# A six-layer cross network on one core: biases transposed by VectorE, remainder loads on two queues, first layer by column groups

## The chip, the core and the metric

The kernel runs on one core of one Trainium2 chip. TensorE (PE) multiplies into eight banks of PSUM (128 partitions x 512 fp32 each); ScalarE (ACT), VectorE (DVE) and GpSimd (POOL) work element by element; transfers are issued from SyncE's queue (SP) or ACT's. Each engine takes its instructions in the order in which the program gives them. The metric is the time of the launch on the device in microseconds (us), the median of several runs; all times below are us.

## What is computed

```python
B, F, D, L = 4096, 26, 16, 6
Din = min(F * D, 1024)          # 416
x0: (B, Din)   ws: (L, Din, Din)   bs: (L, Din)      # all bf16

def reference(x0, ws, bs):
    x = x0
    for l in range(ws.shape[0]):
        x = x0 * (x @ ws[l] + bs[l]) + x
    return x
```

In layer 0, x is x0, so x0 * (x0 @ w + b) + x0 is x0 * (x0 @ w + (b + 1)): the kernel adds 1 to the first layer's bias and leaves the addition out.

## The kernel before, in words

**Layout.** The 416 columns are three blocks of 128 (`NK`, index m for outputs and k for inputs) and a remainder of 32. x is held transposed: `XM[i][:, k, batch]` for the blocks, and `XR[i]` for the remainder, where the 32 columns of four groups of 512 rows lie on the four quarters of the partitions. The 4096 rows are two halves s of 2048, each of four groups of `CW` = 512 (index g). A unit of PE work in the first layer is three matmuls (k) of 128x128 by 128x512 for one output block m and one group: `full` (L222, the matmul on L225). The remainder's part is added by `row` (L228, L232), which multiplies 32 partitions of `XR[0]`, or of `XRx`, a copy with the two 64-partition halves swapped, so that four such matmuls use the four quarters of the array beside each other.

**Loads.** `load_x0t` (L78) fetches 512 rows transposed by DMA, eight times, on SP. `load_xrem` (L83) fetches the 32 remainder columns, 64 bytes a row; those of s = 0 in two pieces of 64 partitions, the first from ACT's queue behind the weights of layer 0 (L99), the second from SP behind the fourth transposed load (L106); those of s = 1 whole (L109). `x0_rem` (L157) makes `XR[0]` and `XRx` of them on DVE: a transpose in 32x32 squares, a copy that reorders, one copy per 64 partitions for `XRx`. All later weights, the rows of x0 for the last layer (`X0rows`, four issues) and the last bias (`bLr`, four issues) follow on SP.

**Biases.** `bias_setup` (L143) transposes the 6x416 biases on PE with an identity matrix that POOL makes (L91): three matmuls and four more for the remainder, into bank 7. DVE adds 1 to the first layer's and copies them to `bM` and `bR` (L151 to L154). ACT reads them per partition.

**Order on PE.** `pe_filler` (L136) runs matmuls on a constant tile from the start: two of 256 columns, nine of 512, then the bias matmuls, and one more of 512. The first layer (`first_layer`, L219) follows for s = 0 and s = 1. A block's result of two groups (one half h of the four) takes a pair of banks, which `two_banks` (L131) hands out in turn, 0, 1, 2, 3. In s = 0, h = 0 goes by groups: (m, group) = (0,0), (1,0), (2,0), (0,1), (1,1), (2,1); h = 1 goes block by block. Six row matmuls close a half. The results of h = 0 are called `pa[m]`, those of h = 1 `pb[m]`.

**Eviction.** `ew_main` (L165) is called for a block and half: ACT reads both banks at once (128x1024), adds the bias and writes bf16 (L168); DVE multiplies by x0 (L171 in layer 0; L173 and L174, with the addition, later). PE may use the pair again when ACT has read it. The remainder's own output is `mm_rem` (L200) and `ew_rem` (L176).

**Later.** Layers 1 to 4 (L300) take six tiles (s, m) of two bank pairs each in the same manner; layer 5 (L385) multiplies with x as the stationary side, so that results come out by rows, and stores them.

Of the kernel before, what the change touches and what calls it, by code (L numbers as in the profile page):

```python
# [16 lines left out]
def kernel(  # L17
# [7 lines left out]
    nc = tc.nc  # L25
# [24 lines left out]
    ident = const.tile([P, P], BF16)  # L50
# [6 lines left out]
    bsb = const.tile([L, D], BF16)  # L57
# [82 lines left out]
    pe_filler(2, 2 * P)  # L140
    pe_filler(9, CW)

    def bias_setup():  # L143
        pb = PS[:, 7, 0:32].rearrange("p (a b) -> p a b", a=4)
        for m in range(NK):
            nc.tensor.matmul(pb[:, m, 0:L], lhsT=bsb[0:L, 128 * m:128 * m + 128], rhs=ident[0:L, 0:L], start=True, stop=True,
                             skip_group_check=True)
        for g in range(NG):
            nc.tensor.matmul(pb[32 * g:32 * g + 32, 3, 0:L], lhsT=bsb[0:L, NK * P:D], rhs=ident[0:L, 0:L], start=True, stop=True,
                             tile_position=(0, 32 * g), skip_group_check=True)  # L150
        nc.vector.tensor_scalar(out=bM[:, :, 0:1], in0=pb[:, 0:NK, 0:1], scalar1=1.0, scalar2=None, op0=ALU.add)  # L151
        nc.vector.tensor_scalar(out=bR[:, 0:1], in0=pb[:, 3, 0:1], scalar1=1.0, scalar2=None, op0=ALU.add)
        nc.vector.tensor_copy(bM[:, :, 1:L], pb[:, 0:NK, 1:L])
        nc.vector.tensor_copy(bR[:, 1:L], pb[:, 3, 1:L])  # L154


    def x0_rem(s, p0, p1):  # L157
        nc.vector.transpose(out=xrt[s][p0:p1], in_=xrem[s][p0:p1])  # L158
        nc.vector.tensor_copy(XR[0][p0:p1, CW * s:CW * s + CW].rearrange("p (j t) -> p j t", t=16),
                              xrt[s][p0:p1].rearrange("p t j -> p j t"))  # L160
        for a in range(p0, p1, 64):
            nc.vector.tensor_copy(XRx[s][64 - a:128 - a, :], XR[0][a:a + 64, CW * s:CW * s + CW])


    def ew_main(l, s, m, h, pt, cur, nxt):  # L165
        c0 = col0(s, 2 * h)
        t = tpool.tile([P, 2 * CW], BF16, name="t")
        nc.scalar.activation(t[:], pt.rearrange("p a b -> p (a b)"), ACT.Identity, bias=bM[:, m, l:l + 1], scale=1.0)  # L168
        x0c = XM[0][:, m, c0:c0 + 2 * CW]
        if l == 0:  # L170
            nc.vector.tensor_tensor(out=nxt[:, m, c0:c0 + 2 * CW], in0=t[:], in1=x0c, op=ALU.mult)  # L171
# [47 lines left out]
    def first_layer(s):  # L219
# [31 lines left out]
        for m in range(NK):  # L251
            ew_main(0, s, m, 0, pa[m], cur, nxt)
        for gl in range(2):
            full(pb[0], 0, 1, gl, s == 0, s == 1)
        if s == 1:
            ew_main(0, s, 0, 1, pb[0], cur, nxt)
        for m in range(1, NK):
            pb.append(two_banks())
            for gl in range(2):
                full(pb[m], m, 1, gl, True, False)  # L260
        if s == 0:
# [3 lines left out]
            x0_rem(1, 0, 128)  # L265
            for m in range(NK):
# [170 lines left out]
```

## Time and profile before

| | us |
|---|---|
| median of three runs (131.67 to 131.97) | 131.84 |
| the profiled execution | 131.1 |
| its span, first to last instruction | 129.3 |
| PE busy | 122.5 |
| DVE busy | 103.1 |
| ACT busy | 83.9 |
| first matmul of the first layer starts | 5.64 |
| first matmul of layer 1 starts | 26.36 |
| last matmul of layer 5 is issued in the piece that ends at | 122.83 |

Times in the rows count from the start of the span. A row of the timeline has start, length, engine, line, operation, output and inputs, and in brackets the idle time of the engine before it and what released it. PEld is the loading of weights into PE; SPq and ACTq are issues of transfers. A row of the groups has the count, the busy time, the mean length in ns, and the idle time before with its releaser.

### The profile page before, as it was taken

To read this page: it belongs to the slowest core of one execution; us is meant where nothing else is said; L and a number is where in the kernel's file an instruction comes from. 1 tells how busy PE (TensorE), PEld (TensorE's weight loads), DVE (VectorE), ACT (ScalarE), POOL (GpSimd) and SP (SyncE) were. 2 spreads that over 40 slices of the span, in tenths; PEclk is the share of its full clock that TensorE was granted. 3 is DMA by queue.
4 is the path that set the end of the run, shared out by engine and by line. 5 is a ranking of instruction groups with operands and counts; after the bars stand their busy time and mean duration, and the time that the engine had idled before them with its cause. 6 is when DMAs were issued, how large, how long until landed. Compare 5 with 4: busy or idle time off the path is not lost.

```text
span 129.3 us, 3927 instructions
## 1 busy us (share of the span) xinstructions
PE 122.5 (95%) x1681; PEld 54.4 (42%) x1683; DVE 103.1 (80%) x186; ACT 83.9 (65%) x92; POOL 5.4 (4%) x18
## 2 busy tenths in 40 slices
PE   6989999999999999999999999999999999999940
PEld 2433343444544444434444544444444345544420
DVE  1163768547989898989898989898989999999990
ACT  0307567598757759756759666849665867567760
POOL 4110000300000000000000000000001200000000
PEclk9999999999999999999999999999999999999997
DMA  3999999999990000000000000000499899996553
GB/s 93 254 213 200 159 182 261 232 329 333 334 298 8 5 0 8 0 0 5 0 5 0 5 0 5 0 5 0 82 126 193 162 138 231 225 312 198 191 172 101
DMA packets 42021, 16.37 MB, mean 127 GB/s; under 512 B 30826, under 2 KB 42004, under 8 KB 42004
## 3 DMA queue, kind: packets, MB, share of 16 engines
q1 hardware_dynamic: 40504, 15.70, 54.5%
q10 hardware_dynamic: 1500, 0.42, 1.7%
q8 instruction: 13, 0.21, 0.7%
q14 instruction: 4, 0.03, 0.1%
HBM read 6.15 MB, written 3.41 MB: 74 GB/s over the span
## 4 chain that ended last, share of the span: by engine, by line
PE 88%; DMA 5%; DVE 1%; ACT 1%; SPq 1%; issue 1%; DVEq 0%
PE PS L190 49%; PE PS L342 12%; PE PS L225 10%; PE PS L196 5%; PE PS L207 5%; DMA XM<-in_x_dram 5%; PE PS L202 2%; PE PS L351 2%; PE PS L232 1%; PE PS L356 1%; SPq L78 1%; DVE t L377 1%; ACT t L168 1%; DVE o L380 1%; ACT t L376 0%
## 5 line engine op out<-in xcount | busy, mean ns | idle before, releaser
L168 ACT ACTIVATE t<-PS,bM 128x1024 bf16<-128x1024 f32 x60 | 62.1, 1114 | 30.8 <-PE PS L196 21.3
L190 PE MATMUL PS<-XM,WM 128*32 128x512 bf16 x1152 | 65.2, 379 | 0.0
L190 PEld LDWEIGHTS <-WM 128*32 128x32 bf16 x1152 | 29.7, 97 | 33.8 <-issue 5.1
L173 DVE TENSOR_TENSOR t<-t,XM 128x1024 bf16<-128x1024 bf16 x48 | 33.3, 694 | 4.2 <-ACT t L168 4.2
L174 DVE TENSOR_TENSOR XM<-t,XM 128x1024 bf16<-128x1024 bf16 x48 | 33.5, 699 | 3.1
L342 PE MATMUL PS<-WM,XM 128*128 128x416 bf16 x96 | 17.9, 340 | 0.0
L225 PE MATMUL PS<-XM,WM 128*128 128x512 bf16 x70 | 16.6, 379 | 0.7 <-DMA XM<-in_x_dram 0.4
L366 ACT CAST t<-PS 128x832 bf16<-128x832 f32 x12 | 10.2, 852 | 5.0 <-PE PS L342 2.5
L342 PEld LDWEIGHTS <-XM 128*128 128x128 bf16 x96 | 8.9, 98 | 8.7 <-issue 2.2
L225 PEld LDWEIGHTS <-WM 128*128 128x128 bf16 x72 | 6.8, 98 | 10.1 <-issue 2.7
L171 DVE TENSOR_TENSOR XM<-t,XM 128x1024 bf16<-128x1024 bf16 x12 | 7.9, 689 | 2.3 <-ACT t L168 2.1
L207 PE MATMUL PS<-XM,WM 128*32 128x512 bf16 x120 | 8.2, 379 | 0.0
L178 ACT ACTIVATE t<-PS,bR 128x512 bf16<-128x512 f32 x10 | 6.8, 694 | 1.4 <-PE PS L207 1.4
L368 DVE TENSOR_TENSOR o<-t,XLrows 128x832 bf16<-128x832 bf16 x12 | 7.1, 592 | 0.5
L196 PE MATMUL PS<-XR,WR 32*128 32x512 bf16 x96 | 7.3, 379 | 0.0
L367 DVE TENSOR_TENSOR t<-t,X0rows 128x832 bf16<-128x832 bf16 x12 | 7.0, 584 | 0.0
L158 DVE STREAM_TRANSPOSE xrt<-xrem 64x512 bf16<-64x512 bf16 (+1 forms) x3 | 2.1, 708 | 5.0 <-DMA xrem<-in_x_dram 5.0
L138 PE MATMUL PS<-warm 128*128 128x512 bf16 (+1 forms) x12 | 4.4, 536 | 1.2 <-DVE warm L89 1.2
L376 ACT CAST t<-PS 128x416 bf16<-128x416 f32 x8 | 4.0, 505 | 1.0 <-PE PS L342 0.8
L207 PEld LDWEIGHTS <-WM 128*32 128x32 bf16 x120 | 3.2, 97 | 3.2
L285 POOL COPY XLrows<-scrR 128x512 bf16<-128x512 bf16 x2 | 1.4, 704 | 74.1 <-DMA scrR<-XR 74.1
L102 DVE COPY WR<-WR 32x416 bf16<-32x416 bf16 x3 | 0.8, 259 | 4.5 <-DMA WR<-in_ws_dram 4.4
(39 smaller groups left out, 42.2 us busy)
## 6 DMA issues: line engine op xcount, KB each, us to landing
X0rows<-in_x_dram SPq DMA_DIRECT2D x4, 832.0 KB, 10.6
out_dram<-o SPq DMA_DIRECT2D x12, 208.0 KB, 2.5
WM<-in_ws_dram SPq DMA_DIRECT2D x5, 312.0 KB
out_dram<-o SPq DMA_DIRECT2D x8, 104.0 KB, 1.8
WR<-in_ws_dram SPq DMA_DIRECT2D x4, 130.0 KB, 5.3
WM<-in_ws_dram ACTq DMA_DIRECT2D x1, 312.0 KB, 3.3
XM<-in_x_dram SPq DMA_TRANSPOSE x8, 4.8
xrem<-in_x_dram SPq DMA_DIRECT2D x1, 128.0 KB
```

The source lines that it names most:

```text
L168: nc.scalar.activation(t[:], pt.rearrange("p a b -> p (a b)"), ACT.Identity, bias=bM[:, m, l:l + 1], scale=1.0)
L171: nc.vector.tensor_tensor(out=nxt[:, m, c0:c0 + 2 * CW], in0=t[:], in1=x0c, op=ALU.mult)
L173: nc.vector.tensor_tensor(out=t[:], in0=t[:], in1=x0c, op=ALU.mult)
L174: nc.vector.tensor_tensor(out=nxt[:, m, c0:c0 + 2 * CW], in0=t[:], in1=cur[:, m, c0:c0 + 2 * CW], op=ALU.add)
L190: nc.tensor.matmul(pts[g // 2][32 * q:32 * q + 32, g % 2, :], lhsT=WM[:, l, k, 128 * m + 32 * q:128 * m + 32 * q + 32], rhs=cur[:, k, c0:c ...
L196: nc.tensor.matmul(pts[g // 2][:, g % 2, :], lhsT=WR[32 * g:32 * g + 32, l, 128 * m:128 * m + 128], rhs=curR[32 * g:32 * g + 32, CW * s:CW ...
L207: nc.tensor.matmul(pr[32 * g:32 * g + 32, :], lhsT=WM[:, l, k, NK * P:D], rhs=cur[:, k, c0:c0 + CW], start=False, stop=(k == NK - 1), tile ...
L225: nc.tensor.matmul(pt[:, gl, :], lhsT=WM[:, 0, k, 128 * m:128 * m + 128], rhs=cur[:, k, c0:c0 + CW], start=(first and k == 0), stop=(last ...
L342: nc.tensor.matmul(py[g // 2][:, g % 2, 0:D], lhsT=cur[:, k, q_cols(q, g)], rhs=WM[:, l, k, :], start=(first and k == 0), stop=((not first ...
L366: nc.scalar.copy(tv, py[h][:, :, 0:D])
L367: nc.vector.tensor_tensor(out=tv, in0=tv, in1=X0rows[:, b0:b0 + 5:4, :], op=ALU.mult)
L368: nc.vector.tensor_tensor(out=o[:], in0=tv, in1=XLrows[:, b0:b0 + 5:4, :], op=ALU.add)
```

## The change

- **Biases.** `bsb` grows to 32 partitions, POOL zeroes it, the biases are loaded into its first six. DVE transposes it in 32x32 squares into `bT`; POOL copies from there to `bM` (four copies) and `bR` (four) and adds 1 to the first layer's. The identity, `bias_setup` and the filler behind it go.
- **Loads.** The first half of the remainder rows of s = 0 is issued by SP as third transfer, behind two transposed loads. The second half is issued by ACT behind its part of the first `x0_rem`. `X0rows` and `bLr` are one issue each.
- **`x0_rem`** takes a list of engines: the first half of s = 0 is transposed and reordered in two pieces, one copy on ACT and one on DVE.
- **First layer.** h = 1 of s = 0 goes by groups as h = 0 does. The rows are closed in the order 0, 2, 1 and the blocks evicted in that order. In s = 1, h = 1 takes (0,0), (1,0), (0,1), (1,1), (2,0), (2,1) and evicts block 0 in between. The bank pairs follow a list, `first_order`, and then the turn 2, 1, 3, 0.
- **`split_first`** evicts block 0 of a half by two engines: ACT the first bank as before, DVE the second bank directly, (PSUM + bias) * x0 in one operation; DVE's multiply for ACT's half is 512 columns. It is used for h = 0 of both s, and for h = 1 of s = 0.
- **Fillers.** Three of 128 columns, nine of 512, one of 256; the constant tile is filled in pieces of 128 and 384 columns.

```diff
-    bsb = const.tile([L, D], BF16)
+    bsb = const.tile([R, D], BF16)
+    bT = const.tile([R, D // R, R], BF16)
...
-    make_identity(nc, ident[:])
+    nc.gpsimd.memset(bsb[:], 0.0)
...
-    nc.scalar.dma_start(bsb[:], bs[:, :])
+    nc.scalar.dma_start(bsb[0:L, :], bs[:, :])
     load_wr(nc.scalar, 0, 0, 1)
-    load_xrem(nc.scalar, 0, 0, 64)
     nc.scalar.activation(dz[:, 1:2], dz[:, 0:1], ACT.Identity, bias=dz[:, 0:1], scale=1.0)
+    nc.vector.transpose(out=bT[:], in_=bsb.rearrange("p (c r) -> p c r", r=R))
+    for q in range(4):
+        nc.gpsimd.tensor_copy(bM[32 * q:32 * q + 32, :, :], bT[:, q:4 * NK:4, 0:L])
+    nc.gpsimd.tensor_scalar(out=bM[:, :, 0:1], in0=bM[:, :, 0:1], scalar1=1.0, scalar2=None, op0=ALU.add)
+    for g in range(NG):
+        nc.gpsimd.tensor_copy(bR[32 * g:32 * g + 32, :], bT[:, 4 * NK, 0:L])
+    nc.gpsimd.tensor_scalar(out=bR[:, 0:1], in0=bR[:, 0:1], scalar1=1.0, scalar2=None, op0=ALU.add)
     for g in range(1, NG):
         nc.vector.tensor_copy(WR[32 * g:32 * g + 32, 0, :], WR[0:32, 0, :])
     load_x0t(0, 1)
+    load_xrem(nc.sync, 0, 0, 64)
     load_x0t(0, 2)
     load_x0t(0, 3)
-    load_xrem(nc.sync, 0, 64, 128)
     load_x0t(1, 0)
     load_x0t(1, 1)
     load_xrem(nc.sync, 1, 0, 128)
...
-    for q in range(4):
-        nc.sync.dma_start(X0rows[:, 8 * q:8 * q + 8, :], x0_v[:, 8 * q:8 * q + 8, :])
-    for g in range(NG):
-        nc.sync.dma_start(bLr[32 * g:32 * g + 1, :], bs[LL:LL + 1, :])
+    nc.sync.dma_start(X0rows[:], x0_v)
+    nc.sync.dma_start(bLr[0:P:32, :], bs[LL:LL + 1, :].broadcast_to([NG, D]))
...
+    first_order = [0, 1, 2, 3, 0, 2, 1, 3, 0, 2, 1, 0, 3]
     def two_banks():
-        i = 2 * (turn[0] % 4)
+        n = turn[0]
+        i = first_order[n] if n < len(first_order) else (2, 1, 3, 0)[(n - len(first_order)) % 4]
         turn[0] += 1
-        return PS[:, i:i + 2, :]
+        return PS[:, 2 * i:2 * i + 2, :]
...
-    pe_filler(2, 2 * P)
+    pe_filler(3, P)
     pe_filler(9, CW)
-    def bias_setup():
...
+    pe_filler(1, 2 * P)
-    def x0_rem(s, p0, p1):
-        nc.vector.transpose(out=xrt[s][p0:p1], in_=xrem[s][p0:p1])
-        nc.vector.tensor_copy(XR[0][p0:p1, CW * s:CW * s + CW].rearrange("p (j t) -> p j t", t=16),
-                              xrt[s][p0:p1].rearrange("p t j -> p j t"))
+    def x0_rem(s, p0, p1, parts):
+        XRv = XR[0][p0:p1, CW * s:CW * s + CW].rearrange("p (j t) -> p j t", t=16)
+        n = 16 // len(parts)
+        for a, copy in enumerate(parts):
+            nc.vector.transpose(out=xrt[s][p0:p1, n * a:n * a + n, :], in_=xrem[s][p0:p1, n * a:n * a + n, :])
+            copy(XRv[:, :, n * a:n * a + n], xrt[s][p0:p1, n * a:n * a + n, :].rearrange("p t j -> p j t"))
         for a in range(p0, p1, 64):
             nc.vector.tensor_copy(XRx[s][64 - a:128 - a, :], XR[0][a:a + 64, CW * s:CW * s + CW])
...
+    def split_first(s, m, h, pt, nxt):
+        c0 = col0(s, 2 * h)
+        t = tpool.tile([P, 2 * CW], BF16, name="t")
+        nc.scalar.activation(t[:, 0:CW], pt[:, 0, :], ACT.Identity, bias=bM[:, m, 0:1], scale=1.0)
+        nc.vector.scalar_tensor_tensor(out=nxt[:, m, c0 + CW:c0 + 2 * CW], in0=pt[:, 1, :], scalar=bM[:, m, 0:1],
+                                       in1=XM[0][:, m, c0 + CW:c0 + 2 * CW], op0=ALU.add, op1=ALU.mult)
+        nc.vector.tensor_tensor(out=nxt[:, m, c0:c0 + CW], in0=t[:, 0:CW], in1=XM[0][:, m, c0:c0 + CW], op=ALU.mult)
...
         row(pa[0], 0, 0, 0, False)
-        row(pa[1], 1, 0, 1, False)
-        row(pa[2], 2, 0, 0, False)
         if s == 1:
             row(pb[0], 0, 1, 0, True)
+        row(pa[2], 2, 0, 0, False)
+        row(pa[1], 1, 0, 1, False)
+        split_first(s, 0, 0, pa[0], nxt)
         if s == 0:
-            x0_rem(0, 64, 128)
-        for m in range(NK):
+            x0_rem(0, 64, 128, (nc.vector.tensor_copy,))
+        for m in (2, 1):
             ew_main(0, s, m, 0, pa[m], cur, nxt)
-        for gl in range(2):
-            full(pb[0], 0, 1, gl, s == 0, s == 1)
-        if s == 1:
-            ew_main(0, s, 0, 1, pb[0], cur, nxt)
-        for m in range(1, NK):
-            pb.append(two_banks())
-            for gl in range(2):
-                full(pb[m], m, 1, gl, True, False)
+        pb += [two_banks() for m in range(1, NK)]
+        for m, gl in ((0, 0), (1, 0), (2, 0), (0, 1), (1, 1), (2, 1)) if s == 0 else ((0, 0), (1, 0), (0, 1), (1, 1), (2, 0), (2, 1)):
+            full(pb[m], m, 1, gl, s == 0 or m > 0, s == 1 and m == 0)
+            if s == 1 and (m, gl) == (0, 1):
+                ew_main(0, s, 0, 1, pb[0], cur, nxt)
         if s == 0:
             row(pb[0], 0, 1, 0, False)
             row(pb[1], 1, 1, 0, False)
             row(pb[2], 2, 1, 1, False)
-            x0_rem(1, 0, 128)
-            for m in range(NK):
+            split_first(s, 0, 1, pb[0], nxt)
+            x0_rem(1, 0, 128, (nc.vector.tensor_copy,))
+            for m in range(1, NK):
                 ew_main(0, s, m, 1, pb[m], cur, nxt)
...
-    bias_setup()
-    pe_filler(1, CW)
-    x0_rem(0, 0, 64)
+    x0_rem(0, 0, 64, (nc.scalar.copy, nc.vector.tensor_copy))
+    load_xrem(nc.scalar, 0, 64, 128)
```

More of the change, by code (lines that the diff above doesn't have):

```diff
@@ L48 @@
     out_v = out.rearrange("(bt p) d -> p bt d", p=P)
-    ident = const.tile([P, P], BF16)
     dz = const.tile([P, 2], FP32)
@@ L63 @@
     scrR = [big.tile([P, 4, P], BF16, name=f"scrR{s}") for s in range(NS)]
+    xrt = [big.tile([P, 16, R], BF16, name=f"xrt{s}") for s in range(NS)]
     xrem = [big.tile([P, 16, R], BF16, name=f"xrem{s}") for s in range(NS)]
-    xrt = [big.tile([P, 16, R], BF16, name=f"xrt{s}") for s in range(NS)]
     XRx = [big.tile([P, CW], BF16, name=f"XRx{s}") for s in range(NS)]
@@ L86, in load_wr @@
         eng.dma_start(WR[32 * g:32 * g + 32, l0:l1, :], ws[l0:l1, NK * P:D, :].rearrange("l r n -> r l n"))
-    for a in range(2):
-        nc.vector.memset(warm[:, 2 * P * a:2 * P * a + 2 * P], 0.5)
+    nc.vector.memset(warm[:, 0:P], 0.5)
+    nc.vector.memset(warm[:, P:CW], 0.5)
     nc.vector.memset(dz[:], 0.0)
-    make_identity(nc, ident[:])
+    nc.gpsimd.memset(bsb[:], 0.0)
     nc.gpsimd.memset(ones[:], 1.0)
```

20 lines of the change are left out of this document (2 added, 18 removed).

## The prediction

> **What bounds the kernel now.** I read the page first (span, busy shares, chain), then the chain of waits in order of time, then the timeline of the first 30 us engine by engine.
>
> ```profile
> span 129.3 us, 3927 instructions
> PE 122.5 (95%) x1681; PEld 54.4 (42%) x1683; DVE 103.1 (80%) x186; ACT 83.9 (65%) x92; POOL 5.4 (4%) x18
> PE 88%; DMA 5%; DVE 1%; ACT 1%; SPq 1%; issue 1%; DVEq 0%
> ```
>
> PE is the bound. The chain (start, length, what) shows the few places where something else holds it:
>
> ```profile
> 2.17 5.92 DMA XM<-in_x_dram
> ...
> 8.13 2.10 PE PS L225 x9
> ...
> 15.27 1.12 ACT t L168
> ...
> 16.44 3.40 PE PS L225 x15
> ...
> 26.54 2.59 PE PS L190 x48
> ...
> 122.19 0.65 PE PS L342 x3
> ```
>
> From 16.44 to 122.83 the chain is PE alone. Whatever PE saves before 26.4, where layer 1 begins, moves the end by as much; nothing else in the diff can. So the study is of this PE timeline:
>
> ```profile
> 5.14 0.22 PE L146 MATMUL PS<-ident,bsb 6*128 6x6 bf16 x3
> 5.41 0.39 PE L138 MATMUL PS<-warm 128*128 128x512 bf16 x1
> 5.64 2.11 PE L225 MATMUL PS<-XM,WM 128*128 128x512 bf16 x9
> 8.13 2.10 PE L225 MATMUL PS<-XM,WM 128*128 128x512 bf16 x9 [0.39 <-DMA XM<-in_x_dram]
> 10.16 0.39 PE L232 MATMUL PS<-XR,WR 32*128 32x512 bf16 x2
> 10.70 4.21 PE L225 MATMUL PS<-XM,WM 128*128 128x512 bf16 x17
> 14.84 0.39 PE L232 MATMUL PS<-XR,WR 32*128 32x512 bf16 x2
> 15.38 0.82 PE L225 MATMUL PS<-XM,WM 128*128 128x512 bf16 x3
> 16.44 3.40 PE L225 MATMUL PS<-XM,WM 128*128 128x512 bf16 x15 [0.24 <-ACT t L168]
> 20.31 4.06 PE L225 MATMUL PS<-XM,WM 128*128 128x512 bf16 x17
> ```
>
> Nine matmuls in 2.10 with a last one of 0.38 are (2.10 - 0.38) / 8 = 0.215 us each, 0.65 per column group of one block. Two holes: the nine at 5.64 are issued by 7.58, and the next wait until 8.13 for the second transposed load (0.55); the three at 15.38 are through at 16.03, and PE waits until 16.44 (0.41) for ACT to empty the banks of the block before. I call the two starts of row matmuls R0 = 10.16 and T1 = 14.84.
>
> **Part 1: biases by VectorE.** Seven bias matmuls and a filler leave PE between 5.14 and 5.64. First load:
>
> ```profile
> DMA to landing us min/median/max: 4.8/4.8/4.8
> ```
>
> It is issued at 0.73 and lands at 5.53, so real work can start at most 0.1 sooner, and then waits for the second load anyway: I count 0. The shorter filler leaves PE idle for a few tenths ahead of 5.6; the hole at 8.13 is as long, and the nine behind it take 2.10 as those ahead took 2.11. What the new path costs, from the groups by form:
>
> ```profile
> L124 POOL COPY WD<-WR 32x32 bf16<-32x32 bf16 x4 | 0.9, 222 | 4.0 <-DMA WR<-in_ws_dram 3.8
> L158 DVE STREAM_TRANSPOSE xrt<-xrem 64x512 bf16<-64x512 bf16 x2 | 1.4, 706 | 3.2 <-DMA xrem<-in_x_dram 3.2
> L159 DVE COPY XR<-xrt 64x512 bf16<-64x512 bf16 x2 | 1.2, 588 | 0.1
> ```
>
> The biases have landed by 5.14 (the bias matmuls read them). A transpose of 32x416 is at most 0.71, so POOL starts by 5.85. Its eight copies of up to 32x18 and two adds lie between the smallest POOL spans (0.1) and the 0.22 above; at 0.3 each with semaphores bM is complete at 7.4, all at 8.9. ACT first needs bM at about 10.2. Cover: 2.8 us; nothing until a POOL step costs 0.9. WR's three copies come behind the transpose on DVE and end by 6.8, ahead of the remainder rows.
>
> **Part 2: the loads.** On SP the first half of the remainder rows (call its landing L) goes from ACT's queue to third place, behind two transposed loads. Now:
>
> ```profile
> 2.17 2.69 SPq L78 DMA_TRANSPOSE XM<-in_x_dram  x1
> 2.27 0.63 ACTq L83 DMA_DIRECT2D xrem<-in_x_dram  x1
> 4.91 3.50 SPq L78 DMA_TRANSPOSE XM<-in_x_dram  x2
> 6.59 1.82 SPq L78 DMA_TRANSPOSE XM<-in_x_dram  x1
> 8.46 0.68 SPq L83 DMA_DIRECT2D xrem<-in_x_dram  x1
> 9.18 2.21 SPq L78 DMA_TRANSPOSE XM<-in_x_dram  x1
> DMA to landing us min/median/max: 4.9/4.9/4.9
> DMA to landing us min/median/max: 4.4/4.4/4.4
> DMA to landing us min/median/max: 3.4/3.4/3.4
> ```
>
> The three landing rows belong to the issues at 6.59, 9.18 and 8.46: landings at 11.49, 13.58 and 11.9. Between the first load (5.53) and the fourth (11.49) a load takes 1.99 on average; the second took 2.56 (to 8.09), and the 64 KB of remainder rows landed in its interval, at 7.87. Taken off, the second should land near 5.53 + 1.99 = 7.52 (bounds: 2.17 + 4.4 = 6.57, and 8.09 as now). Then PE goes on at 7.6 and could reach the rows at 7.6 + 2.03 = 9.63.
>
> L: its issue takes the slot at 4.91, so 4.91 + 3.4 = 8.3; or 0.4 behind the transposed load ahead of it, as 11.9 stands to 11.49, so 7.9 to 8.5. I take 8.4; the upper bound is the transposed loads' 4.9, L = 9.8. DVE then:
>
> ```profile
> 7.87 0.70 DVE L158 STREAM_TRANSPOSE xrt<-xrem 64x512 bf16<-64x512 bf16 x1 [0.77 <-DMA xrem<-in_x_dram]
> 8.61 0.58 DVE L159 COPY XR<-xrt 64x512 bf16<-64x512 bf16 x1
> 9.22 0.29 DVE L162 COPY XRx<-XR 64x512 bf16<-64x512 bf16 x1
> ```
>
> Today XR is there 1.35 after the landing. Split, DVE makes two transposes and one copy of 256 columns: 2 x 0.35 + 0.29 = 1.0 if time halves with size, 2 x 0.71 + 0.58 = 2.0 if it doesn't shrink. With a fixed 0.15 (as between 0.69 for 1024 and 0.42 for 512 columns of multiply, below) it is 2 x 0.46 + 0.37 = 1.3: again 1.35, XRx 0.3 later, hidden by the four row matmuls ahead of it. ACT's copy (half of 0.69 plus overhead) and its issue of the second half (0.63) end near L + 1.65; ACT's first eviction starts at L + 1.35 + 0.44: hidden by 0.1. So R0 = max(9.63, L + 1.35) = 9.75. **Gain at R0: 0.41.**
>
> The third and fourth loads come a place later: 7.5 + 2.1 (the spacing 11.49 to 13.58, which also has remainder rows in it) = 9.6 and 11.6, needed at about 10.5 and 12.6. The second half's issue is at about L + 1.0 = 9.4 instead of 8.46; landing 3.4 later, 12.8, XR at 14.15, needed at T1 = 14.6: hidden by 0.45 (rival C). What else follows on SP keeps its bytes ahead of it. X0rows in one issue and bLr in one are needed past 103: 0.
>
> **Part 3: order and split evictions.** The prices:
>
> ```profile
> 10.60 3.12 ACT L168 ACTIVATE t<-PS,bM 128x1024 bf16<-128x1024 f32 x3 [6.08 <-PE PS L232]
> ...
> 25.73 0.69 ACT L178 ACTIVATE t<-PS,bR 128x512 bf16<-128x512 f32 x1 [1.40 <-PE PS L207]
> 26.31 1.11 ACT L168 ACTIVATE t<-PS,bM 128x1024 bf16<-128x1024 f32 x1
> ```
>
> ```profile
> L171 DVE TENSOR_TENSOR XM<-t,XM 128x1024 bf16<-128x1024 bf16 x12 | 7.9, 689 | 2.3 <-ACT t L168 2.1
> L181 DVE TENSOR_TENSOR XR<-t,XR 128x512 bf16<-128x512 bf16 x2 | 0.8, 422 | 1.4 <-ACT t L178 1.4
> ```
>
> ACT starts 0.44 after the rows begin; a half block takes 0.69 and the next starts 0.58 after it, a whole one 1.11.
>
> By column groups, PE in the second half of s = 0 reaches block 2 after two groups of 0.65. Its bank pair is now that of pa[2], the second one that ACT empties: R0 + 0.44 + 0.58 + 1.11 + 0.05 = R0 + 2.18. PE is there at R0 + 0.54 (rows) + 0.1 + 1.3 = R0 + 1.94, so a **new wait** of 0.24 comes in; behind it stand 12 matmuls (2.58) and 0.1 to the rows, T1 = R0 + 4.86 against 14.84 - 10.16 = 4.68 now. **Loss 0.18.** The same wait hides up to 0.24 of a late third load.
>
> At T1 the split empties half of pb[0]'s pair at T1 + 0.44 + 0.69 + 0.05 = T1 + 1.18; PE wants it at T1 + 0.54 + 0.65 = T1 + 1.19. The 0.41 at 16.44 is gone. **Gain 0.41.** DVE's half is an operation that the trace has not: PSUM in, add and multiply at once. Bounds 0.42 (the multiply of that size) and 1.11 (ACT's whole block); near ACT's 0.69 for the same PSUM read. PE needs that half at T1 + 0.54 + 9 x 0.215 = T1 + 2.5, DVE comes to it behind two multiplies at T1 + 1.1: even 1.11 is covered.
>
> What is late next: with s = 1, T1 = 14.6, the eight loads. The last one is needed in the before at 20.31 + 0.65 = 20.96, without a wait; in the new order only after six matmuls of the half, 20.31 - 0.64 + 1.3 = 20.97. The rest of the first layer on PE has no hole in either version. Layer 1 gets the same relabelled bank pairs.
>
> **Sum.** 0.41 - 0.18 + 0.41 = 0.64. The profiled execution took 131.1 (1.8 around its span of 129.3) and gives 130.46; the median of the runs shown is 131.84, 0.74 above the profiled one, and gives **131.2**. In terms of L: gain = 9.04 - L, at most 0.78 (R0 not under 9.63).
>
> **The rivals.**
>
> **A, a part of it**: L between 8.6 and 9.04, or the split chain on DVE nearer to 2.0 than 1.35. R0 between 9.95 and 10.4, gain 0 to 0.45: 131.4 to 131.85. For it: ACT's copy has two semaphores more in the chain. Against: the SP queue's own remainder load took 3.4.
>
> **B, slower: the first rows come too late.** In SP's queue the rows cannot pass the second transposed load, as they do today (7.87 against 8.09, issued 0.1 after it). If the queue serves them like the transposed loads, 4.9 after the issue, L = 9.8 and the gain is 9.04 - 9.8 = -0.76: 132.6. It decides from L = 9.04 on. The Trainium skill, "DMA: Bandwidth & Descriptors", section "Queues, rings and completion order", has it that an engine takes the descriptors of one ring in order and goes round-robin between the rings of different issuers; by that rule the move gives up a parallel ring for a place in a line. That the two loads landed 0.2 apart agrees with the round-robin.
>
> **C, slower: the second rows come too late.** On ACT's queue the remainder load took 7.87 - 2.27 = 5.6 from issue to landing. At that price the second half lands at 15.0 and XR is there at 16.35, T1 slips by 1.75 and the gain turns to -1.1: 132.95. It begins to cost from a landing at 13.25 and decides from 13.9. Against it: ahead of the 5.6 stood 300 KB of weights in the same queue, which is empty by then.
>
> **D, no change**: the split doesn't free the pair sooner (DVE or ACT late by the new order), the 0.41 stays, the gain is 0.23: 131.6.
>
> **How the numbers follow.** A measurement of this kernel can tell about 0.2%, 0.26 us, from no change. Forecast (gain 0.45 to 0.78) 0.50; A 0.20, half of it over 0.26 (L up to 8.78); B 0.10; C 0.10; D 0.10. Faster: 0.50 + 0.10 = 0.60. Same: half of A and D, 0.20. Slower: 0.20. The range reaches down to the cap, 131.84 - 0.78 and 0.15 for the spread of the runs (131.67 to 131.97): 130.9; up over A and D with the same spread: 132.0; it leaves out B and C. The forecast's own range is 130.9 to 131.5.
>
> **What would show it.** The second group's first matmul at 7.6 to 7.8 (not 8.13); the first row transpose on DVE near 8.4; rows at 9.75; a new idle of about 0.2 ahead of PE's seventh matmul in the second half, released by ACT; no wait for ACT in s = 1. Wrong if DVE waits for the first remainder half until past 9.0, if rows at T1 wait for the second half, or if the bias copies on POOL end past 10.

## The result and the profile after

| | before | changed |
|---|---|---|
| median of six runs (lowest to highest) | 131.91 (131.67 to 132.14) | 130.93 (130.53 to 131.23) |
| the profiled execution | 131.1 | 130.53 |
| its span | 129.3 | 128.7 |
| first matmul of layer 1 starts | 26.36 | 26.06 |

The change is faster: 0.9923 of the time before, 95% interval 0.9903 to 0.9944. By the forecast it was 131.2 / 131.84 = 0.995. On the base of the prediction the ratio makes 0.9923 x 131.84 = 130.82, just under the low end of the range, 130.9. (A ratio here is the recorded one of the runs beside each other; it isn't the quotient of the two medians and can differ from it by 0.002.) So the direction was right and the gain was larger, 0.98 instead of 0.64.

The page of the changed kernel, span and busy time by engine:

```profile
span 128.7 us, 3923 instructions
PE 122.9 (95%) x1677; PEld 54.5 (42%) x1677; DVE 104.2 (81%) x187; ACT 83.3 (65%) x93; POOL 7.0 (5%) x27
```

PE is still the bound, and its timeline over the first layer is the place to look. The changed kernel:

```profile
1.04 4.61 PE L146 MATMUL PS<-warm 128*128 128x128 bf16 x13 [1.04 <-DVE warm L88]
5.52 4.42 PE L232 MATMUL PS<-XM,WM 128*128 128x512 bf16 x18
9.88 0.39 PE L239 MATMUL PS<-XR,WR 32*128 32x512 bf16 x2
...
10.41 1.50 PE L232 MATMUL PS<-XM,WM 128*128 128x512 bf16 x6
12.11 2.75 PE L232 MATMUL PS<-XM,WM 128*128 128x512 bf16 x12 [0.20 <-ACT t L166]
14.79 0.39 PE L239 MATMUL PS<-XR,WR 32*128 32x512 bf16 x2
...
15.32 4.06 PE L232 MATMUL PS<-XM,WM 128*128 128x512 bf16 x18
19.32 0.60 PE L239 MATMUL PS<-XR,WR 32*128 32x512 bf16 x6
...
19.86 4.20 PE L232 MATMUL PS<-XM,WM 128*128 128x512 bf16 x18
...
26.06 2.76 PE L197 MATMUL PS<-XM,WM 128*32 128x512 bf16 x48
```

Read it against the PE rows of before. The rows start at 9.88 instead of 10.16 (R0). The seventh matmul of the next half waits for ACT, as forecast. T1 is 14.79 against 14.84: what was won at R0 is gone again. The 18 matmuls from 15.32 are unbroken: 4.06, where before had a hole after three. The 18 from 19.86 have 0.14 of waiting in them.

VectorE in the changed kernel, the steps whose prices were open:

```profile
4.64 0.60 DVE L101 STREAM_TRANSPOSE bT<-bsb 32x416 bf16<-32x416 bf16 x1 [3.24 <-DMA bsb<-in_bs_dram]
...
7.92 0.76 DVE L157 STREAM_TRANSPOSE xrt<-xrem 64x256 bf16<-64x256 bf16 x2 [1.35 <-DMA xrem<-in_x_dram]
...
10.39 0.75 DVE L179 SCALAR_TENSOR_TENSOR XM<-PS,bM,XM 128x512 bf16<-128x512 f32 x1 [0.91 <-PE PS L239]
...
12.67 0.71 DVE L157 STREAM_TRANSPOSE xrt<-xrem 64x512 bf16<-64x512 bf16 x1 [1.16 <-DMA xrem<-in_x_dram]
```

The landing column of the transfers and SP's rows have the first remainder half earlier still:

```profile
2.18 2.57 SPq L78 DMA_TRANSPOSE XM<-in_x_dram  x1
...
4.80 0.67 SPq L83 DMA_DIRECT2D xrem<-in_x_dram  x1
```

```profile
XM<-in_x_dram SPq DMA_TRANSPOSE x1, 4.7
...
xrem<-in_x_dram SPq DMA_DIRECT2D x1, 64.0 KB, 3.1
```

The two rows belong to the issues at 2.18 and 4.80: the second transposed load is there at 2.18 + 4.7 = 6.9 and the rows at 4.80 + 3.1 = 7.9 (L). The second remainder half has landed by 12.67, and DVE's half of an eviction takes 0.75, inside its bounds of 0.42 and 1.11. POOL's rows, bias and remainder bias with the 1 added:

```profile
6.43 0.24 POOL L104 TENSOR_SCALAR bM<-bM 128x3 f32<-128x3 f32 x1
...
7.55 0.22 POOL L107 TENSOR_SCALAR bR<-bR 128x1 f32<-128x1 f32 x1
```

bM is complete by 6.67, 3.7 before ACT's first eviction at 10.36, and bR by 7.77.

**A way to read all runs.** The same marks were taken in every profile: R0, T1, then T2 and T3, the starts of the row matmuls that close the two halves of s = 1 (19.77 and 24.30 in before), and L1, the first matmul of layer 1. A half without any wait takes 4.53 from mark to mark (many rows below), and T3 to L1 is 2.06 in each. What is over 4.53 is time that PE stood. The last column is the profiled execution's time less L1: all that comes after the first layer.

| profile | R0 | T1-R0 | T2-T1 | T3-T2 | L1 | time | time-L1 |
|---|---|---|---|---|---|---|---|
| before | 10.16 | 4.68 | 4.93 | 4.53 | 26.36 | 131.10 | 104.74 |
| e1, before | 10.24 | 4.67 | 4.92 | 4.84 | 26.73 | 131.47 | 104.74 |
| e9, before | 10.27 | 4.53 | 4.93 | 4.53 | 26.32 | 131.09 | 104.77 |
| e13, before with one issue each | 10.16 | 4.53 | 4.92 | 5.15 | 26.82 | 131.28 | 104.46 |
| changed | 9.88 | 4.91 | 4.53 | 4.68 | 26.06 | 130.53 | 104.47 |
| e5, changed | 9.69 | 5.06 | 4.94 | 4.95 | 26.70 | 131.14 | 104.44 |
| e10, changed | 9.45 | 5.38 | 4.53 | 4.64 | 26.07 | 130.50 | 104.43 |
| e14, changed | 10.06 | 4.91 | 4.54 | 4.84 | 26.41 | 130.98 | 104.57 |
| e11, changed, eight issues | 9.73 | 4.91 | 4.87 | 4.76 | 26.33 | 131.03 | 104.70 |
| e2, loads undone | 10.26 | 4.91 | 4.53 | 4.53 | 26.29 | 130.84 | 104.55 |
| e16, loads undone | 10.12 | 4.91 | 4.53 | 4.53 | 26.15 | 130.60 | 104.45 |
| e3, split undone | 9.97 | 5.47 | 4.92 | 4.93 | 27.35 | 131.84 | 104.49 |
| e17, order of s = 1 undone | 9.64 | 4.92 | 5.08 | 5.31 | 27.01 | 131.47 | 104.46 |
| e4, biases undone | 9.68 | 5.30 | 4.63 | 4.54 | 26.21 | 130.88 | 104.67 |
| e15, biases undone | 9.70 | 5.39 | 4.64 | 4.86 | 26.65 | 131.34 | 104.69 |
| e6, old fillers | 9.71 | 5.48 | 4.53 | 4.89 | 26.67 | 131.16 | 104.49 |
| e7, loads alone | 10.62 | 5.39 | 4.93 | 4.53 | 27.53 | 132.28 | 104.75 |
| e8, two more steps | 9.47 | 5.67 | 4.80 | 4.53 | 26.53 | 131.03 | 104.50 |
| e12, block 2 split | 9.54 | 4.83 | 4.62 | 5.00 | 26.05 | 130.53 | 104.48 |
| e18, loads undone, block 2 split | 10.24 | 4.55 | 4.53 | 5.06 | 26.44 | 130.95 | 104.51 |

### The profile page after: what moved, and what is told of

It is laid out like the page before. It is cut to its first block, busy times and chain, and to the rows that moved or that the text cites. A ratio compares the mean times of both kernels' runs of the same rounds, so it can differ in the third digit from the quotient of the medians.

```text
span 128.7 us, 3923 instructions
## 1 busy us (share of the span) xinstructions
PE 122.9 (95%) x1677; PEld 54.5 (42%) x1677; DVE 104.2 (81%) x187; ACT 83.3 (65%) x93; POOL 7.0 (5%) x27
## 4 chain that ended last, share of the span: by engine, by line
PE 93%; ACT 2%; DVE 2%; issue 1%; DVEq 0%; ACTq 0%
PE PS L197 49%; PE PS L342 12%; PE PS L232 12%; PE PS L203 5%; PE PS L214 5%; PE PS L146 4%; PE PS L209 2%; PE PS L351 2%; PE PS L239 1%; PE PS L356 1%; DVE t L377 1%; ACT t L166 1%; DVE o L380 1%; ACT t L178 1%; ACT t L376 0%
## 5 line engine op out<-in xcount | busy, mean ns | idle before, releaser
L166 ACT ACTIVATE t<-PS,bM 128x1024 bf16<-128x1024 f32 x57 | 59.1, 1115 | 21.2 <-PE PS L203 21.2
L172 DVE TENSOR_TENSOR XM<-t,XM 128x1024 bf16<-128x1024 bf16 x48 | 33.5, 698 | 3.1
L169 DVE TENSOR_TENSOR XM<-t,XM 128x1024 bf16<-128x1024 bf16 x9 | 5.9, 688 | 1.5 <-ACT t L166 1.5
L146 PE MATMUL PS<-warm 128*128 128x512 bf16 (+2 forms) x13 | 4.6, 535 | 1.0 <-DVE warm L88 1.0
L178 ACT ACTIVATE t<-PS,bM 128x512 bf16<-128x512 f32 x3 | 2.1, 687 | 5.3 <-PE PS L239 5.3
L157 DVE STREAM_TRANSPOSE xrt<-xrem 64x256 bf16<-64x256 bf16 (+2 forms) x4 | 2.2, 562 | 3.5 <-DMA xrem<-in_x_dram 3.5
```

Source lines behind the costliest of these rows:

```text
L146: nc.tensor.matmul(PS[:, 0, 0:cols], lhsT=warm[:, 0:P], rhs=warm[:, 0:cols], start=True, stop=True, skip_group_check=True)
```

## The experiments

The theory after the result: the gain of 0.98 is the wait behind ACT (0.41) and something that the sum had at nothing. Its rivals are the loads, the biases, the order of s = 1, or something behind the first layer. Each run has its own runs of before beside it on the same chip. Medians of different chips are not compared, ratios are.

**e1, before again.** No edit.

> The kernel before, unchanged, profiled a second time: the profiled execution of before took 131.1 us, 0.8 under its median of 131.91. Theory 1 (the first layer's loads and bank waits explain the gain, the profile is typical): rows of the first half of s = 0 start again at 10.2 and the ones behind at 14.8, layer 1 at 26.4. Theory 2 (that profile was a lucky one, and an ordinary execution loses more in the first layer): the rows start at 10.4 to 11, layer 1 at 26.7 to 27.2. Theory 3 (the executions differ behind layer 1, in the last loads or the stores): the same 26.4, and the span longer at its end.

131.43 against 131.41, ratio 1.0008 [0.9979, 1.0037]. The PE timeline of this execution, the piece that was unbroken in the first profile of before (`20.31 4.06 ... x17`):

```profile
20.38 4.36 PE L225 MATMUL PS<-XM,WM 128*128 128x512 bf16 x17
```

Here 0.30 of waiting is inside it. The first profile had none there, so at this place it was a favourable execution of before.

**e2 and e16, the loads back in their old places.**

```diff
     load_wr(nc.scalar, 0, 0, 1)
+    load_xrem(nc.scalar, 0, 0, 64)
...
-    load_xrem(nc.sync, 0, 0, 64)
     load_x0t(0, 2)
     load_x0t(0, 3)
+    load_xrem(nc.sync, 0, 64, 128)
...
-    load_xrem(nc.scalar, 0, 64, 128)
```

> The changed kernel with the remainder loads where they were (first half on ACT's queue behind the weights, second half on SP behind the fourth transposed load). Theory 1: rows at 10.2 instead of 9.9 (+0.3), but the last transposed load lands 0.4 sooner and its wait of 0.15 goes: ratio to before 0.993 to 0.995 against 0.992. Theory 2 (the loads cost an ordinary execution of before more than its profile showed): 0.997 to 1.000.

> The changed kernel with the remainder loads where they were, beside the change on one chip. Theory 1 (the rows start 0.3 to 0.4 later, given back in part at the last transposed load): 0.15 to 0.35 us slower than the change. Rival (the loads carry nothing): within 0.1 us of it.

e2: 130.67 against 131.41, 0.9943 [0.9921, 0.9965]. e16: 130.77 against 131.62, 0.9925 [0.9896, 0.9953]; the changed kernel beside it on the same chip (e14) 0.9939 [0.9914, 0.9964]. Moving the loads is worth nothing that can be told. PE of e16:

```profile
8.08 2.10 PE L233 MATMUL PS<-XM,WM 128*128 128x512 bf16 x9 [0.44 <-DMA XM<-in_x_dram]
10.12 0.39 PE L240 MATMUL PS<-XR,WR 32*128 32x512 bf16 x2
...
12.35 2.75 PE L233 MATMUL PS<-XM,WM 128*128 128x512 bf16 x12 [0.20 <-ACT t L167]
15.03 0.39 PE L240 MATMUL PS<-XR,WR 32*128 32x512 bf16 x2
...
20.10 4.06 PE L233 MATMUL PS<-XM,WM 128*128 128x512 bf16 x18
```

The wait for the second load is back and R0 is 0.24 later than in the changed kernel, yet the last piece is unbroken, and L1 is 26.15 against 26.06. The last transposed load was issued at 16.31 here and landed at 21.02; in e2 it landed at 21.43, and in four profiles of the change at 21.27 to 21.92. So what the move wins at R0 can be lost at that load.

**e3, the split evictions undone**, `split_first` replaced by `ew_main`.

```diff
-        split_first(s, 0, 0, pa[0], nxt)
+        ew_main(0, s, 0, 0, pa[0], cur, nxt)
...
-            split_first(s, 0, 1, pb[0], nxt)
+            ew_main(0, s, 0, 1, pb[0], cur, nxt)
```

> The changed kernel with every block evicted by ACT alone. Theory 1: the wait at the seventh matmul of the second half grows from 0.2 to about 0.65, and the wait for the pair of the first block comes back (0.4): 0.85 us lost of 0.98, ratio to before 0.998 to 1.000. Theory 2 (the loads carry the gain): 0.993 to 0.996.

131.50 against 131.41, 1.0011 [0.9988, 1.0034]: without it nothing is left of the gain. PE of e3:

```profile
11.62 0.81 PE L232 MATMUL PS<-XM,WM 128*128 128x512 bf16 x3 [0.22 <-ACT t L166]
12.63 2.75 PE L232 MATMUL PS<-XM,WM 128*128 128x512 bf16 x11 [0.20 <-ACT t L166]
...
21.96 3.40 PE L232 MATMUL PS<-XM,WM 128*128 128x512 bf16 x14 [0.23 <-ACT t L166]
```

By column groups PE comes back to a pair sooner, and without the split it waits at each of these places. In the half from 16.09 to 20.36 its fourth matmul starts at 17.03, 0.28 late, when ACT is done with the pair (the timeline starts no row for idle time that short). The split pays for the order, not only for itself.

**e4 and e15, the biases on PE again**, with the old fillers: `bias_setup`, the identity and the filler behind it come back, DVE's transpose and POOL's copies go.

```diff
-    nc.vector.transpose(out=bT[:], in_=bsb.rearrange("p (c r) -> p c r", r=R))
...
-    pe_filler(3, P)
+    pe_filler(2, 2 * P)
     pe_filler(9, CW)
-    pe_filler(1, 2 * P)
...
+    bias_setup()
+    pe_filler(1, CW)
     x0_rem(0, 0, 64, (nc.scalar.copy, nc.vector.tensor_copy))
```

> The changed kernel with the biases transposed by PE and the old fillers. Theory 1: the first load sets the start of the first layer's matmuls at 5.5 in both, so nothing: ratio 0.991 to 0.994 as for the change. A rival (the bias matmuls kept PE from the first load, or their PSUM reads on DVE delayed the rows): 0.995 to 0.998.

> The changed kernel with the biases transposed by PE and the old fillers, beside the change on one chip. Theory 1 (bias matmuls and a filler hold PE back from the first load when the clock rises late): first layer from 5.6 to 6.1 instead of 5.5, and 0.2 to 0.5 us slower than the change. Rival (no part of the gain, the earlier run was another chip's): within 0.15 us of the change.

e4: 131.21 against 131.41, 0.9967 [0.9945, 0.9989]. e15: 131.37 against 131.62, 0.9987 [0.9959, 1.0016], and the changed kernel beside e15 on the same chip 0.9939 [0.9914, 0.9964]; e4 had no run of the change beside it. So the biases seem to be worth 0.0028 to 0.0048 of 131.6, 0.4 to 0.6, though the intervals overlap in part. The fillers, undone with them, are tried by themselves in e6. PE and DVE of e15:

```profile
15.09 0.61 PE L246 MATMUL PS<-XR,WR 32*128 32x512 bf16 x4 [0.47 <-DVE XR L165]
```

```profile
13.71 0.71 DVE L164 STREAM_TRANSPOSE xrt<-xrem 64x512 bf16<-64x512 bf16 x1 [2.44 <-DMA xrem<-in_x_dram]
```

The second remainder half has landed only by 13.71 (12.67 in the changed kernel, 12.86 in e14). This is rival C's mechanism, at T1. But it does not reach layer 1: L1 is 26.21 and 26.65, inside the 26.06 to 26.70 of the change. What the two profiles do show is behind the first layer, 104.67 and 104.69 against 104.43 to 104.57. There DVE stands for 0.46 ahead of a multiply of layer 5, and the profile shows nothing that it waits for. First e4, then the changed kernel at the same multiply:

```profile
108.40 0.59 DVE L377 TENSOR_TENSOR o<-t,XLrows 128x832 bf16<-128x832 bf16 x1 [0.46 <-issue]
```

```profile
107.89 0.59 DVE L368 TENSOR_TENSOR o<-t,XLrows 128x832 bf16<-128x832 bf16 x1
```

e15 has the same 0.46 at 108.86. DVE's last instruction then ends 99.8 behind L1 in both, and 99.7 in the changed kernel's first profile. So 0.1 to 0.2 of the 0.4 to 0.6 is found. Why DVE stands there, and where the rest is, stays open.

**e5, e10 and e14, the changed kernel again**, each beside what it is compared with.

> The changed kernel, unchanged, as the reference for the runs beside it. Ratio to before 0.990 to 0.994 again. Its profile: first matmul of the first layer at 5.5, rows at 9.5 to 10.3 (9.5 if the clock rises early, up to 0.8 later if late), a wait of 0.2 at the seventh matmul of the second half.

> The changed kernel once more, as the reference for the two beside it: ratio to before 0.990 to 0.995; start of layer 1 plus 104.47.

> The changed kernel as the reference for the three beside it: ratio 0.991 to 0.994.

130.91 against 132.00, 0.9929 [0.9903, 0.9955]; 130.51 against 131.29, 0.9929 [0.9905, 0.9953]; 130.92 against 131.62, 0.9939 [0.9914, 0.9964]. On 131.84, these ratios make a gain of 0.80 to 0.94. PE of e10:

```profile
5.48 4.04 PE L232 MATMUL PS<-XM,WM 128*128 128x512 bf16 x18
9.45 0.39 PE L239 MATMUL PS<-XR,WR 32*128 32x512 bf16 x2
...
12.80 2.10 PE L232 MATMUL PS<-XM,WM 128*128 128x512 bf16 x9 [0.30 <-DMA XM<-in_x_dram]
14.83 0.39 PE L239 MATMUL PS<-XR,WR 32*128 32x512 bf16 x2
```

R0 is 0.43 earlier than in the first profile of the change, and T1 no earlier: the fourth transposed load is there at 12.80, not at the 11.6 of the prediction. Whatever PE wins ahead of it ends there.

**e6, the old fillers alone** in the changed kernel (2 of 256, 9 of 512, 1 of 512 columns).

```diff
-    pe_filler(3, P)
+    pe_filler(2, 2 * P)
     pe_filler(9, CW)
-    pe_filler(1, 2 * P)
+    pe_filler(1, CW)
```

> The changed kernel with the old fillers (two of 256, nine of 512, one more of 512) and without the bias matmuls. Theory 1 (the filler and bias matmuls on PE hold the first layer back whenever the clock rises late, since the loads no longer hide it): the first layer's matmuls start 0.1 to 0.4 later, ratio 0.994 to 0.997 as with the biases undone. Theory 2 (undoing the biases cost time by another way, the second half of the remainder rows landing late): as the change, 0.990 to 0.994.

131.16 against 132.00, 0.9933 [0.9906, 0.9959], beside e5's 0.9929: the fillers are no part of it.

**e7, the loads moved in before**, without ACT's copy in `x0_rem`.

```diff
     load_wr(nc.scalar, 0, 0, 1)
-    load_xrem(nc.scalar, 0, 0, 64)
...
     load_x0t(0, 1)
+    load_xrem(nc.sync, 0, 0, 64)
...
-    load_xrem(nc.sync, 0, 64, 128)
...
     x0_rem(0, 0, 64)
+    load_xrem(nc.scalar, 0, 64, 128)
```

> The kernel before with the remainder loads moved alone. Theory 1: the second transposed load lands at 6.9 instead of 8.1, PE's start (5.6 to 6.0) and not the load then sets the rows, 9.7 to 10.1 instead of 10.2; the wait of 0.4 behind ACT stays and the last transposed load comes 0.4 later: ratio 0.997 to 1.001. Theory 2 (the loads carry most of the gain): 0.993 to 0.996.

132.27 against 132.00, 1.0021 [1.0000, 1.0043]. It does not measure what its name says. ACT has nothing to do ahead of its issue, so the second half is issued at 2.34, beside the second transposed load. ACT's queue and PE of e7:

```profile
2.34 0.63 ACTq L83 DMA_DIRECT2D xrem<-in_x_dram  x1
```

```profile
8.58 2.10 PE L224 MATMUL PS<-XM,WM 128*128 128x512 bf16 x9 [0.35 <-DMA XM<-in_x_dram]
...
12.68 3.40 PE L224 MATMUL PS<-XM,WM 128*128 128x512 bf16 x15 [0.71 <-DMA XM<-in_x_dram]
```

PE gets the second transposed load at 8.58 and the fourth at 12.68. In the change, ACT's copy is also what keeps the issue back until 8.40.

**e8 and e12, two more steps on top of the change.** e12 splits block 2 of s = 0 too; e8 does that and issues the remainder rows of s = 1 from ACT.

```diff
+        if s == 0:
+            split_first(s, 2, 0, pa[2], nxt)
```

> The changed kernel, with block 2 of the first half evicted by two engines as well, and the remainder rows of s = 1 issued by ACT behind those of s = 0 instead of by SP. Theory 1: the wait of 0.2 at the seventh matmul and that of 0.15 for the last transposed load go: 0.2 to 0.35 us faster than the change, ratio 0.988 to 0.991. Against it: the two remainder loads share ACT's queue with the transposed loads, and if rows then wait at 14.8, 0.992 to 0.996.

> The changed kernel with block 2 of the first half of s = 0 evicted by two engines as well. Theory 1: the wait at the seventh matmul of the second half (0.2) goes, if the third load isn't late: 0.1 to 0.2 us faster than the run of the change beside it. Rival: that wait only gives its place to a wait for the fourth transposed load or for the second half of the remainder rows: no difference.

e8: 131.36 against 132.00, 0.9954 [0.9936, 0.9973], if anything slower than e5's 0.9929 beside it. (The transposed loads are on SP's queue in e8 too, not on ACT's as the expectation has it.) e12: 130.62 against 131.29, 0.9931 [0.9905, 0.9957], beside e10's 0.9929: no difference. PE of e8:

```profile
13.11 2.10 PE L231 MATMUL PS<-XM,WM 128*128 128x512 bf16 x9 [0.74 <-DMA XM<-in_x_dram]
```

The wait for ACT is gone, and the fourth load, now at 13.11, takes its place.

**e9, before, a third profile**, beside e10.

> The kernel before, profiled a third time. In every profile so far the time is the start of layer 1 plus a constant, 104.74 for before and 104.47 for the change. Theory 1: its start of layer 1 differs from 26.4 and 26.7 by holes that stand at waits for transposed loads (the third block row of the halves), 0.3 to 0.8 in all, and the constant is 104.74 again. Rival: the difference stands at PE's start or behind the first layer.

131.09, with 131.29 (130.91 to 131.99) for the runs beside it. L1 is 26.32 and the constant 104.77: as in the first profile, with no wait for the last load.

**e11 and e13, the last loads.** e11 is the changed kernel with four issues for `X0rows` and four for `bLr`; e13 is before with one issue for each and no other edit:

```diff
-    for q in range(4):
-        nc.sync.dma_start(X0rows[:, 8 * q:8 * q + 8, :], x0_v[:, 8 * q:8 * q + 8, :])
-    for g in range(NG):
-        nc.sync.dma_start(bLr[32 * g:32 * g + 1, :], bs[LL:LL + 1, :])
+    nc.sync.dma_start(X0rows[:], x0_v)
+    nc.sync.dma_start(bLr[0:P:32, :], bs[LL:LL + 1, :].broadcast_to([NG, D]))
```

> The changed kernel with X0rows and the last bias in four issues each, as before. Theory 1 (the number of issues on SP decides where SP pauses among the last stores): the fifth-last to last stores come 0.2 to 0.3 later, the constant behind layer 1 is 104.74, ratio 0.002 above the run of the change beside it. Rival (the end differs for another reason): as the run of the change beside it.

> The kernel before with X0rows and the last bias in one issue each, and nothing else. Theory 1 (six issues fewer on SP move a pause of SP out of the last stores): the last stores come 0.2 to 0.3 sooner behind the last multiply, time less start of layer 1 is 104.47 instead of 104.74, ratio 0.998. Rival (the end differs by something else in the change): 104.74, ratio 1.000.

e11: 130.96 against 131.29, 0.9970 [0.9951, 0.9989] (e10 beside it 0.9929). e13: 131.49 against 131.62, 0.9968 [0.9945, 0.9991]. The time after L1 goes to 104.70 in e11 and to 104.46 in e13: by this edit it switches between the value of before and that of the change, in both directions. The place is the last stores on SP. Before, and then the changed kernel:

```profile
124.08 0.33 SPq L381 DMA_DIRECT2D out_dram<-o  x1
...
124.65 0.33 SPq L381 DMA_DIRECT2D out_dram<-o  x1
...
125.52 0.34 SPq L381 DMA_DIRECT2D out_dram<-o  x1
```

```profile
124.34 0.33 SPq L381 DMA_DIRECT2D out_dram<-o  x1
...
124.92 0.33 SPq L381 DMA_DIRECT2D out_dram<-o  x1
...
125.49 0.34 SPq L381 DMA_DIRECT2D out_dram<-o  x1
```

The results come every 0.57. In before, one store is issued 0.87 after the one ahead of it, in the change 0.57. e11 has the 0.87 (124.62 to 125.49), e13 has not (125.11 to 125.68).

The trace's own records of SP, which have its waiting instructions too, say more. In before they are empty from 124.99 to 125.45, and so for 0.46 in all five profiles with eight issues. The record behind the gap, the 80th of SP, asks for the end of a store that had landed at 121.16, so SP was not held by that. In all twenty profiles a packet of instructions (8 KB) is fetched 0.2 to 0.7 behind this 80th record. The DMA view has it, in before between 124 and 127, and in the changed kernel only between 127 and 129.3:

```profile
q14 instruction: 1, 0.01, 0.9%
```

```profile
q14 instruction: 1, 0.01, 1.3%
```

With eight issues the 80th record stands between the last stores, with two it stands behind the last one (127.18 in the changed kernel, store at 125.93), where SP has only landings to wait for. That SP stands still because it goes over to newly fetched instructions there is argued from this; no run tests it.

And e13's first layer, which is that of before, has the longest wait for the last load among the four profiles of this first layer:

```profile
20.16 0.82 PE L223 MATMUL PS<-XM,WM 128*128 128x512 bf16 x3
21.43 3.40 PE L223 MATMUL PS<-XM,WM 128*128 128x512 bf16 x15 [0.45 <-DMA XM<-in_x_dram]
```

Three matmuls are through at 20.16 + 0.65 = 20.81, and the next starts at 21.43: 0.62.

**e17, the order of the last half undone** in the changed kernel, block by block as in before.

```diff
-        for m, gl in ... else ((0, 0), (1, 0), (0, 1), (1, 1), (2, 0), (2, 1)):
+        for m, gl in ... else ((0, 0), (0, 1), (1, 0), (1, 1), (2, 0), (2, 1)):
```

> The changed kernel, with the second half of s = 1 multiplied block by block again, (0,0), (0,1), (1,0), so that the last transposed load is needed 0.65 us sooner. Theory 1 (in ordinary executions that load lands late, and the new order hides most of it): a wait of 0.5 to 0.9 for it at the fourth matmul of that half, 0.3 to 0.7 us slower than the change, ratio 0.995 to 0.999. Rival (the order of that half doesn't matter): 0.992 to 0.994 as the change.

131.73 against 132.11, 0.9982 [0.9957, 1.0008]; the changed kernel has 0.9923 to 0.9939 elsewhere. PE of e17:

```profile
19.64 0.60 PE L239 MATMUL PS<-XR,WR 32*128 32x512 bf16 x6 [0.46 <-DVE XR L158]
...
20.28 0.82 PE L232 MATMUL PS<-XM,WM 128*128 128x512 bf16 x3
21.62 3.40 PE L232 MATMUL PS<-XM,WM 128*128 128x512 bf16 x15 [0.52 <-DMA XM<-in_x_dram]
```

The last load is again needed after three matmuls, and PE stands until 21.62, 0.69 after the three are through. With six matmuls ahead of it the changed kernel stands only 0.11 to 0.42 in that half (T3-T2 of 4.64 to 4.95). The wait of 0.46 ahead of it, for the remainder rows of s = 1, is no part of this edit; e5 has it too (0.24).

**e18, a version put together from these**: the change with the loads undone and block 2 split.

> The changed kernel with the remainder loads where they were, and block 2 of the first half of s = 0 evicted by two engines as well. Theory 1: with the fourth load back at 11.5, the wait of 0.2 at the seventh matmul of the second half goes: 0.1 to 0.25 us faster than with the loads undone alone (0.9925 and 0.9943), ratio 0.990 to 0.993. Rival (the wait moves to another place): 0.992 to 0.995.

130.60 against 132.11, 0.9905 [0.9868, 0.9943]. It is the best ratio of all, but its interval holds that of the change: not shown to be better. PE of e18:

```profile
10.77 4.09 PE L233 MATMUL PS<-XM,WM 128*128 128x512 bf16 x18
```

The new wait is gone, T1 - R0 is 4.55, and T3 - T2 is 5.06: in that execution the last load took back what was won.

## Why the prediction was right and wrong

**Where the gain is.** The mean marks of four first layers of before (before, e1, e9, e13) and five of the change (changed, e5, e10, e14, e11). The last row leaves out e13 and e11:

| | before | changed | difference | forecast |
|---|---|---|---|---|
| R0 | 10.21 | 9.76 | -0.45 | -0.41 |
| T1-R0 | 4.60 | 5.03 | +0.43 | +0.18 |
| T2-T1 | 4.93 | 4.68 | -0.24 | -0.41 |
| T3-T2 | 4.76 | 4.77 | +0.01 | 0 |
| after L1 (three with eight issues, four with two) | 104.75 | 104.48 | -0.27 | 0 |

The sum is -0.52. The timed runs give 0.80 to 1.02. The rest, 0.3 to 0.5, is in no profile: the three profiled executions of before itself took 131.09 to 131.47, while the medians of before beside them were 131.91, 131.41 and 131.29; four profiled executions of the change took 130.50 to 131.14 at medians of 130.51 to 130.93. The slower executions of before, up to 132.0 or more beside every profiled one, were never profiled. What they wait for is argued only: the last load, needed after three matmuls, cost 0.62 in e13 and 0.69 in e17 by the same order.

**What ends the first layer.** The last transposed load lands at 21.27, 21.92, 21.28 and 21.62 in the profiles of the changed kernel, e5, e10 and e14 (issue plus the time to landing), and T3 follows 2.72 to 2.73 behind it in each, and in e6, e12, e15 and e18 too. So in the change this load decides when layer 1 begins, and a few tenths won at R0, T1 or T2 are lost in the wait for it. By the order of before T3 stands 3.37 behind the landing where PE waits for it (e13, e17): the new order is worth 0.64 in such an execution.

**Step by step.**

- *R0 = 9.75, gain 0.41*: the mean is right, 9.76 (9.45 to 10.06), but by another way, and so in part by luck. The second load is there at 6.8 to 7.1, not 7.52, and L, where the trace has it, is 7.9 to 8.4. PE's own 18 matmuls, which start at 5.5 to 5.8 and don't stop for the second load in any of the five profiles, decide R0; only in e5 is L + 1.35 (8.35 + 1.35 = 9.70) as late as they are. Rival B fell: in the first profile the rows landed as early in line behind two transposed loads as they had on ACT's queue. They did not pass the second load, as B had it: they landed 1.0 to 1.3 behind it.
- *The third and fourth loads at 9.6 and 11.6*: failed. Where PE waits for them it goes on at 10.54 (e5) and 12.80 (e10). With the new wait this gives back the whole of R0: T1-R0 grew by 0.43, not 0.18. e2 and e16, without the move, are as fast.
- *The new wait, T1 = R0 + 4.86*: right in sum, 4.91 wherever the loads are in time, by two misses that nearly cancel. The wait is 4.91 - 4.53 = 0.38, not 0.24, and the half without it is 4.53, not 4.86 - 0.24 = 4.62. e12 and e18 take the wait away, and the fourth or the last load is late instead. The 4.68 of before was no half without waits either: 0.15 of it is a wait for the fourth load.
- *The 0.41 at 16.44 gone*: right. T2-T1 is 4.92 or 4.93 in every profile of before and 4.53 in three of five of the change (in e5 and e11 the remainder rows of s = 1 are late instead, marked 0.24 and 0.25); e3 brings 0.28 of it back, for ACT. Rival D fell.
- *The second remainder rows, hidden by 0.45*: mostly. 12.67 was forecast as 12.8; in e5 they are at 13.36, in e15 at 13.71, where T1 pays 0.47. Rival C's mechanism is there, at a size of tenths.
- *Biases, "I count 0"*: not settled. bM is in time as forecast, but e4 and e15 lose 0.4 to 0.6, of which 0.1 to 0.2 is found on DVE in layer 5.
- *"X0rows in one issue and bLr in one are needed past 103: 0"*, and with it that nothing in the diff but PE's time before 26.4 can move the end: failed. They are needed late, but their number sets when one of the last stores is issued: 0.27, shown by e11 and e13. With it the forecast would have been 130.93 and the low end of the range 130.63. This is the step that put the time out of the range. (The 122.83 of the table of before is where the chain leaves PE; PE's last matmul starts at 124.06 there, and ACT, DVE and SP end the launch.)
- *The last load, "without a wait"*: failed. That was one execution's luck. e1 and e13 wait 0.30 and 0.62 for it, and all five profiles of the change stand in that half too, by 0.11 to 0.42. The order of the last half, which the sum had at nothing, is worth 0.004 to 0.006 of the time (e17), in runs that were not all on one chip.
- *131.84, "0.74 above the profiled one", carried over to the change*: failed as a step of its own. The distance of the profiled execution to the median was 0.81 for before and 0.40 for the change: a median is not a profile plus a constant when the waits differ between executions.

That the sum for the first layer (0.64) lies near the timed gain without the end (0.98 - 0.27 = 0.71) is not a proof of its terms: one was given back, and another was missing.

## What to carry to other kernels

Before you price a wait, read the same place in several executions: a load that is just in time in one profile is a wait in the next, and an order that needs it later is worth something that the one profile does not show. A gain ahead of a chain of loads ends at the first load that is late, so the landings are to be followed to the end of the chain. Take the time after the last place that an edit touches as a number of its own: here it should have been a constant, and the fact that it wasn't led to the eight issues.

## What was not expected of the hardware

- With six issues fewer on SP, some 90 to 100 us ahead, SP issues one of the last stores 0.3 earlier. In the five profiles with eight issues SP pauses for 0.46 ahead of its 80th record, and in all twenty a fetch of instructions follows that record; that the one causes the other is not shown.
- The clock of PE. The 18 matmuls without a wait take 4.42 in the changed kernel's first profile and 4.04 in e10, and before's eleven fillers take 4.02 in one execution and 4.36 in another (e1). First before, then e1, on PE:

```profile
1.19 4.02 PE L138 MATMUL PS<-warm 128*128 128x256 bf16 x11 [1.19 <-DVE warm L89]
```

```profile
1.19 4.36 PE L138 MATMUL PS<-warm 128*128 128x256 bf16 x11 [1.19 <-DVE warm L89]
```

  In the changed kernel's first profile the matmuls of 512 columns start 0.38 to 0.43 apart until 6.33 and 0.22 apart behind it; in e10 they are 0.22 apart from 5.48 on. Over all profiles, the last one that starts so late behind another lies 2.5 to 5.8 behind PE's first. The granted clock is 9 in every early slice of these pages, so it does not show this. The Trainium skill, "TensorE: Matmul & The Clock Gate", Part 1, says that the activity window of about 3.4 us runs freely and does not start with the kernel, so that the moment of the rise varies from one execution to the next; the spread of 0.3 to 0.4 here agrees with that.
- The same load is there tenths sooner or later from one execution to the next: the second remainder half landed by 12.67, 12.86 and 13.36 in three executions of the change.
